# The w_sp product of a gMLP block, regrouped by one level of Strassen's scheme

## The chip, the cores and the metric

The kernel runs on one core of a Trainium2 chip. The core has TensorE (PE in the profile: matrix products into PSUM; its weight loads are listed as PEld), VectorE (DVE), ScalarE (ACT), GpSimd (POOL) and SyncE (SP), which here issues most of the DMAs. Each engine takes its instructions in order from a queue of its own; semaphores tie the queues together. The metric is the device time of one execution in microseconds (us); less is better.

## The reference

The module is a chain of two blocks with a residual around each. The first (an S4D convolution over 2048 positions, 512 channels) isn't touched by the change. The second is the gMLP mixer:

```python
def _B_ref(x, w_in, w_sp, b_sp, w_out):        # x: (1, 2048, 512), layer-normed
    Fh = F // 2                                 # F = 1792, Fh = 896
    z = _gelu(jnp.einsum("bsd,df->bsf", x, w_in))
    z1 = z[..., :Fh]
    z2 = _layernorm(z[..., Fh:], axis=-1)
    g = jnp.einsum("ts,bsf->btf", w_sp, z2) + b_sp[None, :, None]
    return jnp.einsum("bsf,fd->bsd", z1 * g, w_out)
```

The product in the line of g is the largest of the kernel: w_sp is 2048 x 2048, z2 is 2048 x 896. Everything is float32.

## The kernel before

**Stages.** The first block runs from the start of the profile to about 352 us; then phase_b1 (the rest of it, layer norm, transposes, and the half z1 of the first mixer product), phase_b2 (the other half, z2, with GELU and layer norm) and phase_b3 (the product with w_sp, the gate, the product with w_out, the stores). The change is in the end of phase_b2 and in phase_b3.

**Products in three parts.** A float32 operand is split into a rounded part `hi` and a remainder `lo`, both in a format (float32r) that TensorE takes at a higher rate. `split` (lines 917 to 919) is a cast on ScalarE and a subtraction on VectorE. A product is then hi·hi + hi·lo + lo·hi: three matmuls, which the loops over `((0, 0), (0, 1), (1, 0))` write out.

**phase_b2.** Row tile t of 16 (128 positions) gets two halves of 448 features (lines 1070 to 1079). After GELU and the statistics, lines 1083 to 1085 normalise each half in PSUM and split it into `z2[t]`, which holds hi and lo of 896 features. Twelve of the z2 tiles lie in the pool "z", four in the places of the earlier weights ("wa", "wb").

**phase_b3.** g is made transposed: 7 feature tiles (fb) of 128 features by 4 chunks (tch) of 512 output positions. For each chunk, 7 PSUM banks `gs` collect over 16 s-tiles (si) of 128 positions (lines 1151 to 1161). The weights held by TensorE are a 128 x 128 block of z2, the moving operand is a 128 x 512 block of w_sp. `raw(n)` loads such a block into one of 4 raw buffers, `wt(n)` splits it into one of 3 pairs, about 2 steps ahead. When a chunk is complete, its banks get b_sp (`bts`), are multiplied with z1, which is read back from DRAM (`z1s`), and split into `gz`: the gate (lines 1170 to 1183). While the next chunk runs, its steps 4, 7, 10 and 13 each take one block of 21 matmuls with w_out (`wo`), for 128 positions of the chunk before (lines 1162 to 1169); `store` adds the residual and writes the rows out. The last chunk's gate and product come at the end (lines 1186 to 1204); there the odd feature tiles are multiplied on GpSimd.

**Order.** In phase_b2 and phase_b3 the order in each engine's queue is set when the program is built, by a list scheduler that goes by the order of the text and by when it reckons operands to be ready: in the profile ScalarE casts w_out blocks between phase_b2's last tiles. PSUM has 7 banks under the tag "g" and one under "tp" (the blocks with w_out).

Of the kernel before, what the change touches and what calls it, by code (L numbers as in the profile page):

```python
# [22 lines left out]
NL2 = 64  # L23
# [154 lines left out]
class Plan:  # L178
# [738 lines left out]
def split(nc, hi, lo, src):  # L917
    nc.scalar.copy(hi, src)  # L918
    nc.vector.tensor_sub(lo, src, hi.bitcast(F32))  # L919
# [128 lines left out]
def phase_b2(tc, zp, wp, ins, ht, product, bank, mhalf):  # L1048

    nc = tc.nc  # L1050
    w2 = zp.tile([P, 2, 4, FH], F32R, tag="w2", name="w2")
    raw = [zp.tile([P, 2, FH], F32, tag="z", bufs=12, name=f"w2r{i}") for i in range(2)]
# [6 lines left out]
    z2 = [zp.tile([P, 4 * FQ], F32R, tag="z", bufs=12, name=f"z2_{t}") for t in range(12)]  # L1059
    for t in "wa", "wb":  # L1060
        ends = wp.tile([P, 2, 4 * FQ], F32R, tag=t, name=f"z_{t}")
        z2 += [ends[:, 0], ends[:, 1]]
    sms = zp.tile([P, 2, 16], F32, tag="sm", name="sm")
    for t in range(16):

        hi, lo = (ht[t // 4][k][:, :, P * (t % 4):P * (t % 4) + P] for k in range(2))
        sm = sms[:, t % 2]
        zt = z2[t].rearrange("p (k h f) -> p k h f", k=2, h=2)
        pts = []
        for half in range(2):  # L1070
            pt = bank(f"pz2_{t}_{half}", [P, 512])
            f = slice(FQ * half, FQ * half + FQ)
            for q in range(4):
                for i, (a, b) in enumerate(((hi, 0), (hi, 1), (lo, 0))):
                    nc.tensor.matmul(pt[:, :FQ], a[:, q], w2[:, b, q, f], start=(q == 0 and i == 0), stop=(q == 3 and i == 2))  # L1075
            v = pt[:, :FQ]
            nc.scalar.activation(v, v, AF.Gelu_apprx_tanh)
            nc.vector.bn_stats(sm[:, 6 * half:6 * half + 6], v)
# [10 lines left out]
def phase_b3(tc, hp, bp, ins, out, z2, w2, zos, bank, tp, scr):  # L1089

    nc = tc.nc
    z1_d, h_d = scr["z1"], scr["h"]
    NT = 4
    NW = 16 * NT

    def place(n, k, dt, name):
        t = hp.tile([P, 4, 512], dt, tag=f"h{n}{k}", name=name)
        return [t[:, i] for i in range(4)], [t[:, 2 * i:2 * i + 2] for i in range(2)]

    raws, _ = place(0, 0, F32, "raws")  # L1100
    sums = place(0, 1, F32, "sums0")[0] + place(1, 0, F32, "sums1")[0]
    z1s = [sums.pop(), zos[2]]
    wts = place(1, 1, F32R, "wts0")[1]
    w, g = place(2, 0, F32R, "wts1")[1]
    wts.append(w)
    gz = [t for n, k in ((2, 1), (3, 0), (3, 1)) for t in place(n, k, F32R, f"gz{n}{k}")[1]] + [g]
    gts = zos[:2]
    bts = [bp.tile([P, 512], F32, tag=f"bt{i}", name=f"bt{i}") for i in range(2)]
    NB = len(raws)

    def raw(n):
        if n < NW:
            nc.sync.dma_start(raws[n % NB], ins["w_sp"][n // 16, n % 16])

    def wt(n):
        if n < NW:
            split(nc, wts[n % 3][:, 0], wts[n % 3][:, 1], raws[n % NB])
            raw(n + NB)

    def load_b(tch):  # L1120
        nc.sync.dma_start(bts[tch % 2], ins["b_sp"].rearrange("(c o t) -> c o t", c=NT, o=1)[tch].to_broadcast([P, 512]))

    for k in range(NB):
        raw(k)
    wt(0)
    wt(1)
    wo = w2.rearrange("p k q f -> p k (q f)").rearrange("p k (b d) -> p k b d", d=D)
# [4 lines left out]
    for tch in range(2):  # L1132
        load_b(tch)


    ov = out.rearrange("b (a l) d -> (b l) a d", l=NL2)

    def load_h(tch, a, h):
        t0 = 512 * tch + P * a
        nc.sync.dma_start(h, h_d[t0:t0 + P])  # L1140

    def product(pt, a, fb):
        for i, (x, y) in enumerate(((0, 0), (0, 1), (1, 0))):
            nc.tensor.matmul(pt, gz[fb][:, x, P * a:P * a + P], wo[:, y, fb, :], start=(fb == 0 and i == 0), stop=(fb == FB - 1 and i == 2))  # L1144

    def store(tch, a, pt, h):
        nc.vector.tensor_add(h, pt, h)  # L1147
        l0 = 16 * tch + 4 * a
        nc.sync.dma_start(ov[l0:l0 + 4], h)

    for tch in range(NT):
        gs = [bank(f"g{tch}_{fb}", [P, 512]) for fb in range(FB)]
        for si in range(16):
            n = 16 * tch + si
            w = wts[n % 3]
            for fb in range(FB):
                if fb == 4:
                    wt(n + 2)
                f = slice(P * fb, P * fb + P)
                for i, (x, y) in enumerate(((0, 0), (0, 1), (1, 0))):  # L1160
                    nc.tensor.matmul(gs[fb], z2[si][:, x, f], w[:, y], start=(si == 0 and i == 0), stop=(si == 15 and i == 2))  # L1161
            if tch and si in (4, 7, 10, 13):
                a = (si - 4) // 3
                hr = gts[a % 2]
                load_h(tch - 1, a, hr)
                pt = tp(f"po{tch}_{si}", [P, 512])
                for fb in range(FB):
                    product(pt, a, fb)
                store(tch - 1, a, pt, hr)
        if tch < NT - 1:  # L1170
            bt = bts[tch % 2]
            for fb in range(FB):
                if fb % 2:
                    nc.scalar.copy(sums[fb], gs[fb])
                else:
                    nc.vector.tensor_add(sums[fb], gs[fb], bt)
            for fb in range(FB):
                z1 = z1s[fb % 2]
                nc.sync.dma_start(z1, z1_d[tch, fb])
                if fb % 2:  # L1180
                    nc.vector.tensor_add(sums[fb], sums[fb], bt)
                nc.vector.tensor_mul(sums[fb], sums[fb], z1)
                split(nc, gz[fb][:, 0], gz[fb][:, 1], sums[fb])
            if tch + 2 < NT:
                load_b(tch + 2)
    tch = NT - 1
    gl_, h4 = sums, list(gts)
    for a in range(2):
        load_h(tch, a, h4[a])
    for fb in range(FB):  # L1190
        nc.vector.tensor_add(gl_[fb], gs[fb], bts[tch % 2])  # L1191
    pl = [bank(f"pl{a}", [P, 512]) for a in range(4)]
    for fb in range(FB):
        z1 = z1s[fb % 2]
        nc.sync.dma_start(z1, z1_d[tch, fb])
        (nc.gpsimd if fb % 2 else nc.vector).tensor_mul(gl_[fb], gl_[fb], z1)  # L1196
        split(nc, gz[fb][:, 0], gz[fb][:, 1], gl_[fb])
        for a in range(4):
            product(pl[a], a, fb)
# [79 lines left out]
```

## Time and profile before

| | |
|---|---|
| runs | 952.91, 953.44, 953.70 us; median 953.44 |
| profiled execution | span 948.4 us, from the first to the last instruction; its own time isn't listed apart from the runs |
| mean granted TensorE clock | 0.983 |
| stage of the product with w_sp, gate and w_out | from 549.17 us to the end |
| DMA in the whole span | 88.86 MB, mean 94 GB/s |

How to read it: the span is taken by the hardware profiler on the core; the time of a run also holds what lies before the first instruction and after the last. A busy share is an average over stages with different limits, so the stages are read one by one, by windows. The chain that ended last is followed back from the last instruction to what released it.

### The profile page before, as it was taken

To read this page: it belongs to the slowest core of one execution; us is meant where nothing else is said; L and a number is where in the kernel's file an instruction comes from. 1 tells how busy PE (TensorE), PEld (TensorE's weight loads), DVE (VectorE), ACT (ScalarE), POOL (GpSimd) and SP (SyncE) were. 2 spreads that over 40 slices of the span, in tenths; PEclk is the share of its full clock that TensorE was granted. 3 is DMA by queue.
4 is the path that set the end of the run, shared out by engine and by line. 5 is a ranking of instruction groups with operands and counts; after the bars stand their busy time and mean duration, and the time that the engine had idled before them with its cause. 6 is when DMAs were issued, how large, how long until landed. Compare 5 with 4: busy or idle time off the path is not lost.

```text
span 948.4 us, 16818 instructions
## 1 busy us (share of the span) xinstructions
PE 857.6 (90%) x7000; PEld 730.3 (77%) x7000; DVE 525.8 (55%) x939; ACT 387.0 (41%) x623; POOL 241.6 (25%) x206
## 2 busy tenths in 40 slices
PE   1248799999999898899999999999999999999994
PEld 0137688888887898788899988888888888888883
DVE  6987979999988549564168751161116111611141
ACT  5876675887867331534344441131113111311010
POOL 5867475878766100000011100000000000000010
PEclk9999899999999999899999999999999999999997
DMA  9204410410403658452421032142224222422121
GB/s 358 67 1 143 89 28 23 102 31 27 100 2 80 223 226 227 134 135 95 179 72 34 12 111 56 56 128 77 74 67 130 71 78 67 125 74 79 45 69 54
DMA packets 45243, 88.86 MB, mean 94 GB/s; under 512 B 4464, under 2 KB 19568, under 8 KB 42736
## 3 DMA queue, kind: packets, MB, share of 16 engines
q1 hardware_dynamic: 43728, 85.17, 29.5%
q0 software_dynamic: 1440, 2.62, 1.1%
q8 instruction: 55, 0.90, 0.4%
q14 instruction: 20, 0.16, 0.1%
HBM read 59.99 MB, written 19.40 MB: 84 GB/s over the span
## 4 chain that ended last, share of the span: by engine, by line
PE 60%; DVE 1%; issue 0%; ACT 0%
PE g L1161 32%; PE pz L1026 8%; PE pz L1075 8%; PE po L1144 6%; PE y L992 3%; PE pl L1144 2%; DVE w1r L1015 0%; DVE w1r L1013 0%; PE lnh_pm L129 0%; DVE stats L997 0%; DVE raws L1147 0%; DVE xq L995 0%; DVE ht L919 0%; PE lnh_pv L138 0%; ACT big L486 0%
## 5 line engine op out<-in xcount | busy, mean ns | idle before, releaser
L1161 PE MATMUL g<-wts,z 128*128 128x512 f32 x1008 | 233.0, 391 | 0.0
L1161 PEld LDWEIGHTS g<-wts,z 128*128 128x128 f32 x1008 | 189.3, 188 | 41.5
L486 POOL TENSOR_TENSOR wa<-mt 128x512 f32<-128x512 f32 x96 | 149.5, 1581 | 63.8 <-PE ps L486 23.3
L919 DVE TENSOR_TENSOR wts<-raws,wts 128x512 fp32r<-128x512 f32 x64 | 44.1, 689 | 188.9 <-ACT wts L918 188.5
L918 ACT CAST wts<-raws 128x512 fp32r<-128x512 f32 x64 | 39.6, 620 | 256.9 <-PE g L1161 252.9
L1196 POOL TENSOR_TENSOR sums<-sums,zo 128x512 f32<-128x512 f32 x3 | 4.3, 1417 | 365.3 <-DVE sums L1191 359.2
L486 PE MATMUL ps<-big,a 128*128 128x128 f32 (+1 forms) x576 | 72.7, 283 | 11.1 <-ACT trio L486 8.5
L486 PEld LDWEIGHTS ps<-big,a 128*128 128x128 f32 x576 | 67.9, 195 | 15.4 <-ACT trio L486 8.7
L1075 PE MATMUL pz<-w,ht 128*128 128x448 f32 x384 | 77.4, 363 | 0.0
L1075 PEld LDWEIGHTS pz<-w,ht 128*128 128x128 f32 x384 | 72.0, 187 | 5.3
L1026 PE MATMUL pz<-ht,w1h 128*128 128x512 f32 x224 | 71.6, 399 | 0.0
L486 PE MATMUL ps<-c_inv,trio 128*128 128x128 f32 x512 | 62.4, 279 | 1.2 <-DVE f L486 1.1
L486 PEld LDWEIGHTS ps<-c_inv,trio 128*128 128x128 f32 x512 | 58.7, 192 | 4.2 <-DVE f L486 1.7
L486 ACT COPY big<-ps 128x512 f32<-128x512 f32 x74 | 42.8, 584 | 46.3 <-PE ps L486 45.0
L1081 POOL TENSOR_SCALAR sm<-sm 128x1 f32<-128x1 f32 x16 | 3.8, 238 | 223.0 <-DVE sm L1080 223.0
L1144 PE MATMUL po<-w,gz 128*128 128x512 f32 x216 | 52.2, 395 | 0.0
L1026 PEld LDWEIGHTS pz<-ht,w1h 128*128 128x128 f32 x224 | 42.8, 191 | 9.6
L486 ACT ACTIVATE ps<-wb 128x512 f32<-128x512 f32 x64 | 42.9, 687 | 17.0 <-DVE wb L486 15.9
L1144 PEld LDWEIGHTS po<-w,gz 128*128 128x128 f32 x216 | 40.6, 188 | 9.5
L486 DVE TENSOR_TENSOR trio<-ps,trio 128x1024 f32<-128x1024 f32 (+2 forms) x34 | 38.6, 1171 | 12.8 <-PE ps L486 12.7
L486 DVE SCALAR_TENSOR_TENSOR f<-wb,ps 128x1024 f32<-128x1024 f32 x32 | 38.8, 1217 | 12.2 <-ACT wb L486 12.0
L1026 PE MATMUL pz<-ht,w1l 128*128 128x512 f32 x112 | 45.0, 401 | 0.0
(146 smaller groups left out, 1376.0 us busy)
## 6 DMA issues: line engine op xcount, KB each, us to landing
raws<-in_w_sp_dram SPq DMA_DIRECT2D x64, 256.0 KB, 2.7
trio<-trio SPq DMA_DIRECT2D x8, 1024.0 KB, 11.9
g<-in_c_g_dram SPq DMA_DIRECT2D x8, 1024.0 KB, 4.9
scr_z<-zo SPq DMA_DIRECT2D x28, 256.0 KB, 2.0
big<-in_u_a_dram SPq DMA_DIRECT2D x8, 512.0 KB, 9.2
xq<-in_u_b_dram SPq DMA_DIRECT2D x4, 1024.0 KB
scr_h<-xq SPq DMA_DIRECT2D x16, 256.0 KB, 3.9
sums<-scr_z SPq DMA_DIRECT2D x16, 256.0 KB
```

The lines of the kernel that those rows point to most:

```text
L486: r = getattr(getattr(self.nc, e), method)(*[real(x) for x in args], **{k: real(x) for k, x in kw.items()})
L918: nc.scalar.copy(hi, src)
L919: nc.vector.tensor_sub(lo, src, hi.bitcast(F32))
L992: nc.tensor.matmul(py[:, i, :], gt[:, i, r, :], qv[:, r, l0 + i], start=(r == 0), stop=(r == 1))
L1026: nc.tensor.matmul(pt, w[:, q, f], ht[n][k][:, q], start=(q == 0 and i == 0), stop=(q == 3 and i == 2))
L1075: nc.tensor.matmul(pt[:, :FQ], a[:, q], w2[:, b, q, f], start=(q == 0 and i == 0), stop=(q == 3 and i == 2))
L1081: nc.gpsimd.tensor_scalar_add(sm[:, 14:15], sm[:, 13:14], 1e-5)
L1144: nc.tensor.matmul(pt, gz[fb][:, x, P * a:P * a + P], wo[:, y, fb, :], start=(fb == 0 and i == 0), stop=(fb == FB - 1 and i == 2))
L1161: nc.tensor.matmul(gs[fb], z2[si][:, x, f], w[:, y], start=(si == 0 and i == 0), stop=(si == 15 and i == 2))
L1196: (nc.gpsimd if fb % 2 else nc.vector).tensor_mul(gl_[fb], gl_[fb], z1)
```

## The change

The output chunks are taken in pairs p (chunks 2p and 2p + 1), the s-tiles in 8 pairs k (tiles 2k and 2k + 1, `e` and `o` in the code), the features in a left half (tiles 0 to 2, `S1`), a right half (4 to 6, `S2`) and a middle tile (3, `SE`). On these 2 x 2 blocks one level of Strassen's scheme is used: seven products of block sums take the place of eight products of blocks. Products 1, 2, 4 and 7 carry the middle tile along as a fourth feature tile, so that it is a plain product.

- `PRODUCTS` says which two blocks of w (chunk, s-tile) make the moving operand, with which sign, and to which chunk and feature tiles the result is added. `ORDERS` gives the order of the seven for each pair of chunks.
- `z2` is now kept in float32, 8 tiles of two row tiles each; the split in phase_b2 is gone.
- Each of the 112 steps (2 pairs, 7 products, 8 pairs of s-tiles) loads one or two w_sp blocks, sums two on GpSimd and splits the result (`w_prep`), and sums blocks of z2 (on GpSimd in products 3 and 4, on VectorE in 1, 6, 7) and splits that (`z_prep`). w is made 3 steps ahead, z 5. There are 6 raw buffers, 4 pairs for w and 8 for z.
- After each product, VectorE adds its 3 or 4 banks to the float32 sums `cs` (14 tiles, two chunks), the first time together with b_sp.
- `gate` is called as soon as feature tiles of a chunk are complete; its multiplication is on GpSimd (in chunk 3, odd tiles on VectorE).
- The blocks with w_out (`out_part`) wait in a list and are taken at steps 2 and 5 of a product, those of chunk 2 at steps 4 to 7. At the end, w_out's product with tiles 0 to 3 of the last chunk runs ahead of the last gate.

```diff
-        for half, v in enumerate(pts):
-            nc.vector.tensor_scalar(v, v, sm[:, 12:13], sm[:, 15:16], op0=ALU.subtract, op1=ALU.mult)
-            split(nc, zt[:, 0, half], zt[:, 1, half], v)
-    return [z.rearrange("p (k f) -> p k f", k=2) for z in z2], w2
+            o = z2[t // 2][:, t % 2, FQ * half:FQ * half + FQ]
+            nc.vector.tensor_scalar(o, v, sm[:, 12:13], sm[:, 15:16], op0=ALU.subtract, op1=ALU.mult)
+    return z2, w2
...
+S1, SE, S2 = slice(0, 384), slice(384, 512), slice(512, 896)
+LEFT, MID, RIGHT = range(0, 3), range(3, 4), range(4, 7)
+PRODUCTS = {
+    1: dict(w=((0, 0), (1, 1), 1), add=((0, LEFT, 1), (1, RIGHT, 1), (0, MID, 1))),
+    2: dict(w=((1, 0), (1, 1), 1), add=((1, LEFT, 1), (1, RIGHT, -1), (1, MID, 1))),
+    3: dict(w=((0, 0), None, 1), add=((0, RIGHT, 1), (1, RIGHT, 1))),
+    4: dict(w=((1, 1), None, 1), add=((0, LEFT, 1), (1, LEFT, 1), (0, MID, 1), (1, MID, 1))),
+    5: dict(w=((0, 0), (0, 1), 1), add=((0, LEFT, -1), (0, RIGHT, 1))),
+    6: dict(w=((1, 0), (0, 0), -1), add=((1, RIGHT, 1),)),
+    7: dict(w=((0, 1), (1, 1), -1), add=((0, LEFT, 1), (0, MID, 1))),
+}
+ORDERS = ((2, 3, 4, 6, 1, 5, 7), (1, 3, 4, 5, 7, 2, 6))
...
+    def w_prep(n):
+        p, m, k = steps[n]
+        hi, lo = wts[n % NW]
+        rs = mine[n]
+        if len(rs) == 2:
+            op = ALU.add if PRODUCTS[m]["w"][2] > 0 else ALU.subtract
+            nc.gpsimd.tensor_tensor(rs[0], rs[0], rs[1], op=op)
+        split(nc, hi, lo, rs[0])
+
+    def z_prep(n):
+        p, m, k = steps[n]
+        hi, lo = zcs[n % NZ]
+        e, o = z2[k][:, 0], z2[k][:, 1]
+        if m == 2:
+            split(nc, hi, lo, e[:, 0:512])
+            return
+        if m == 5:
+            split(nc, hi[:, :384], lo[:, :384], o[:, S2])
+            return
+        zs = zss[n % 2]
+        w = 512 if m == 4 else 384
+        x, y, op = {1: (e[:, S1], o[:, S2], ALU.add), 3: (e[:, S2], o[:, S2], ALU.subtract),
+                    4: (o[:, 0:512], e[:, 0:512], ALU.subtract), 6: (e[:, S1], e[:, S2], ALU.add),
+                    7: (o[:, S1], o[:, S2], ALU.add)}[m]
+        (nc.gpsimd if m in (3, 4) else nc.vector).tensor_tensor(zs[:, :w], x, y, op=op)
+        split(nc, hi[:, :w], lo[:, :w], zs[:, :w])
+        if m in (1, 7):
+            split(nc, hi[:, SE], lo[:, SE], (e if m == 1 else o)[:, SE])
...
+    def gate(tch, fbs):
+        for fb in fbs:
+            c, z1 = cs[tch % 2][fb], z1s[gated[0] % 2]
+            gated[0] += 1
+            nc.sync.dma_start(z1, z1_d[tch, fb])
+            (nc.vector if tch == 3 and fb % 2 else nc.gpsimd).tensor_tensor(c, c, z1, op=ALU.mult)
+            split(nc, gz[fb][0], gz[fb][1], c)
...
+    AHEAD_Z, AHEAD_W = 5, 3
...
+    for n, (p, m, k) in enumerate(steps):
+        if k == 0:
+            tiles = [x for x in (LEFT if m in (1, 2, 4, 7) else RIGHT)] + ([3] if m in (1, 2, 4, 7) else [])
+            ps = [bank(f"m{p}{m}_{i}", [P, 512]) for i in range(len(tiles))]
+        if n + AHEAD_Z < len(steps):
+            z_prep(n + AHEAD_Z)
+        if n + AHEAD_W < len(steps):
+            w_prep(n + AHEAD_W)
+            load_to(n + AHEAD_W + 2)
+        (whi, wlo), (zhi, zlo) = wts[n % NW], zcs[n % NZ]
+        for j, pt in enumerate(ps):
+            f = slice(P * j, P * j + P)
+            for i, (x, y) in enumerate(((zhi, whi), (zhi, wlo), (zlo, whi))):
+                nc.tensor.matmul(pt, x[:, f], y, start=(k == 0 and i == 0), stop=(k == KT - 1 and i == 2))
+        if todo and k in ((4, 5, 6, 7) if todo[0][0] == 2 else (2, 5)):
+            out_part(*todo.pop(0))
+        if k < KT - 1:
+            continue
+        for half, cols, sign in PRODUCTS[m]["add"]:
+            for i, fb in enumerate(cols):
+                pt, c = ps[3 if cols is MID else i], cs[half][fb]
+                if (p, half, fb) not in begun:
+                    begun.add((p, half, fb))
+                    nc.vector.tensor_tensor(c, bts[half], pt, op=ALU.add if sign > 0 else ALU.subtract)
                 else:
+                    nc.vector.tensor_tensor(c, c, pt, op=ALU.add if sign > 0 else ALU.subtract)
+        u = ORDERS[p].index(m)
+        if p == 0:
+            if m == 4:
+                gate(1, list(LEFT) + list(MID))
+            if m == 1:
+                gate(1, RIGHT)
+                todo += [(1, a) for a in range(4)]
+            if m == 7:
+                for tch in (2, 3):
+                    load_b(tch)
+                gate(0, range(FB))
+                todo += [(0, a) for a in range(4)]
+        else:
+            if m == 5:
+                gate(2, RIGHT)
+            if m == 7:
+                gate(2, list(LEFT) + list(MID))
+                todo += [(2, a) for a in range(4)]
+            if m == 2:
+                gate(3, list(LEFT) + list(MID))
+    tch = 3
     pl = [bank(f"pl{a}", [P, 512]) for a in range(4)]
+    hs = list(gts) + raws[:2]
+    for a in range(4):
+        load_h(tch, a, hs[a])
+    for a in range(4):
+        product(pl[a], a, range(0, 4), True, False)
+    gate(tch, RIGHT)
+    for a in range(4):
+        product(pl[a], a, range(4, 7), False, True)
+        store(tch, a, pl[a], hs[a])
```

More of the change, by code (lines that the diff above doesn't have):

```diff
@@ L1051, in phase_b2 @@
     w2 = zp.tile([P, 2, 4, FH], F32R, tag="w2", name="w2")
-    raw = [zp.tile([P, 2, FH], F32, tag="z", bufs=12, name=f"w2r{i}") for i in range(2)]
+    raw = [zp.tile([P, 2, FH], F32, tag="z", bufs=8, name=f"w2r{i}") for i in range(2)]
     for i in range(2):
@@ L1058, in phase_b2 @@
     product(3)
[L1059 to L1062, printed above, removed]
+    z2 = [zp.tile([P, 2, FH], F32, tag="z", bufs=8, name=f"z2_{k}") for k in range(8)]
     sms = zp.tile([P, 2, 16], F32, tag="sm", name="sm")
@@ L1067, in phase_b2 @@
         sm = sms[:, t % 2]
-        zt = z2[t].rearrange("p (k h f) -> p k h f", k=2, h=2)
         pts = []
@@ L1091, in phase_b3 @@
+ORDERS = ((2, 3, 4, 6, 1, 5, 7), (1, 3, 4, 5, 7, 2, 6))
+def phase_b3(tc, hp, bp, wp, ins, out, z2, w2, zos, bank, tp, scr):
     nc = tc.nc
     z1_d, h_d = scr["z1"], scr["h"]
-    NT = 4
-    NW = 16 * NT
+    KT = 8
     def place(n, k, dt, name):
         t = hp.tile([P, 4, 512], dt, tag=f"h{n}{k}", name=name)
-        return [t[:, i] for i in range(4)], [t[:, 2 * i:2 * i + 2] for i in range(2)]
-    raws, _ = place(0, 0, F32, "raws")
-    sums = place(0, 1, F32, "sums0")[0] + place(1, 0, F32, "sums1")[0]
@@ L1102, in phase_b3 @@
[L1102 to L1106, printed above, removed]
-    gts = zos[:2]
[L1108 to L1118, printed above, removed]
@@ L1120, in load_b, with twos @@
-    def load_b(tch):
[L1121 to L1127, printed above, removed]
+        return [t[:, i] for i in range(4)]
+    def twos(x):
+        return [(x[i], x[i + 1]) for i in range(0, len(x), 2)]
+    raws = place(0, 0, F32, "raws0")
+    x = place(0, 1, F32, "raws1")
+    raws, zss = raws + x[:2], x[2:]
@@ new lines, in phase_b3 @@
+    wts = twos(place(1, 0, F32R, "wts0") + place(1, 1, F32R, "wts1"))
+    x = []
+    for t in "wa", "wb":
+        v = wp.tile([P, 4 * FH], F32R, tag=t, name=f"zc_{t}")
+        x.append([v[:, 512 * i:512 * i + 512] for i in range(7)])
+    zcs = [(x[0][i], x[1][i]) for i in range(7)]
+    gz = twos(place(2, 0, F32R, "gz0") + place(2, 1, F32R, "gz1") + place(3, 0, F32R, "gz2") + place(3, 1, F32R, "gz3"))
+    zcs.append(gz.pop())
+    cs = [bp.tile([P, 512], F32, tag=f"c{i}", name=f"c{i}") for i in range(14)]
@@ new lines, in phase_b3 @@
+    cs = cs[:7], cs[7:]
+    bts = [bp.tile([P, 512], F32, tag=f"bt{i}", name=f"bt{i}") for i in range(2)]
+    z1s = [zos[2], bp.tile([P, 512], F32, tag="z1", name="z1b")]
+    gts = zos[:2]
+    NR, NW, NZ = len(raws), len(wts), len(zcs)
+    steps = [(p, m, k) for p in range(2) for m in ORDERS[p] for k in range(KT)]
+    loads = []
+    for n, (p, m, k) in enumerate(steps):
+        for blk in PRODUCTS[m]["w"][:2]:
+            if blk is not None:
+                loads.append((n, 2 * p + blk[0], 2 * k + blk[1]))
@@ new lines, in phase_b3, with load_to @@
+    mine = {}
+    for r, (n, _, _) in enumerate(loads):
+        mine.setdefault(n, []).append(raws[r % NR])
+    loaded = [0]
+    def load_to(n):
+        while loaded[0] < len(loads) and loads[loaded[0]][0] <= n:
+            r = loaded[0]
+            _, c, si = loads[r]
+            nc.sync.dma_start(raws[r % NR], ins["w_sp"][c, si])
+            loaded[0] += 1
+    def w_prep(n):
[6 more added lines that the diff above has]
+        split(nc, hi, lo, rs[0])
@@ new lines, in phase_b3, with load_h, product @@
+    wo = w2.rearrange("p k q f -> p k (q f)").rearrange("p k (b d) -> p k b d", d=D)
+    ov = out.rearrange("b (a l) d -> (b l) a d", l=NL2)
+    def load_b(tch):
+        nc.sync.dma_start(bts[tch % 2], ins["b_sp"].rearrange("(c o t) -> c o t", c=4, o=1)[tch].to_broadcast([P, 512]))
+    def load_h(tch, a, h):
+        t0 = 512 * tch + P * a
+        nc.sync.dma_start(h, h_d[t0:t0 + P])
+    def product(pt, a, fbs, first, last):
+        for fb in fbs:
+            for i, (x, y) in enumerate(((0, 0), (0, 1), (1, 0))):
+                nc.tensor.matmul(pt, gz[fb][x][:, P * a:P * a + P], wo[:, y, fb, :], start=(first and fb == fbs[0] and i == 0), stop=(last and fb == fbs[-1] and i == 2))
@@ new lines, in store, with out_part @@
+    def store(tch, a, pt, h):
+        nc.vector.tensor_add(h, pt, h)
+        l0 = 16 * tch + 4 * a
+        nc.sync.dma_start(ov[l0:l0 + 4], h)
+    gated = [0]
+    def gate(tch, fbs):
+        for fb in fbs:
+            c, z1 = cs[tch % 2][fb], z1s[gated[0] % 2]
[3 more added lines that the diff above has]
+            split(nc, gz[fb][0], gz[fb][1], c)
+    def out_part(tch, a):
+        hr = gts[a % 2]
+        load_h(tch, a, hr)
+        pt = tp(f"po{tch}_{a}", [P, 512])
+        product(pt, a, range(FB), True, True)
+        store(tch, a, pt, hr)
@@ L1128, in phase_b3 @@
+    AHEAD_Z, AHEAD_W = 5, 3
+    load_to(1)
+    for n in range(AHEAD_Z):
+        z_prep(n)
+        if n < AHEAD_W:
+            w_prep(n)
+            load_to(n + 2)
+    for tch in range(2):
+        load_b(tch)
     for fb in range(FB):
@@ L1131, in phase_b3 @@
         split(nc, wo[:, 0, fb], wo[:, 1, fb], t)
[L1132 to L1174, printed above, removed]
-                else:
[L1176 to L1191, printed above, removed]
-    pl = [bank(f"pl{a}", [P, 512]) for a in range(4)]
[L1193 to L1199, printed above, removed]
@@ L1200, in phase_b3 @@
-    h4 += raws[:2]
-    for a in range(2, 4):
-        load_h(tch, a, h4[a])
-    for a in range(4):
-        store(tch, a, pl[a], h4[a])
+    todo, begun = [], set()
+    for n, (p, m, k) in enumerate(steps):
+        if k == 0:
[21 more added lines that the diff above has]
+                    nc.vector.tensor_tensor(c, bts[half], pt, op=ALU.add if sign > 0 else ALU.subtract)
+                else:
+                    nc.vector.tensor_tensor(c, c, pt, op=ALU.add if sign > 0 else ALU.subtract)
[8 more added lines that the diff above has]
+                for tch in (2, 3):
+                    load_b(tch)
+                gate(0, range(FB))
[8 more added lines that the diff above has]
+                gate(3, list(LEFT) + list(MID))
@@ L1225, in body @@
         bp = es.enter_context(tc.tile_pool(name="b3", bufs=1, reuse_waits="tile"))
-        phase_b3(tc, hp, bp, ins, out, z2, w2, zos, bank, tp, scr)
+        phase_b3(tc, hp, bp, wp, ins, out, z2, w2, zos, bank, tp, scr)
 def layouts(v):
```

1 line of the change is left out of this document (removed).

## The prediction

> **What bounds the kernel now.** I read the page first: the span, the engines' shares and the chain that ended last.
>
> ```profile
> span 948.4 us, 16818 instructions
> PE 857.6 (90%) x7000; PEld 730.3 (77%) x7000; DVE 525.8 (55%) x939; ACT 387.0 (41%) x623; POOL 241.6 (25%) x206
> ...
> PE 60%; DVE 1%; issue 0%; ACT 0%
> ...
> L918 ACT CAST wts<-raws 128x512 fp32r<-128x512 f32 x64 | 39.6, 620 | 256.9 <-PE g L1161 252.9
> ```
>
> (The last row is a group of equal instructions: busy time, mean ns of one, idle time before it and what ended it. A cast of one w tile takes 0.62 us, and ScalarE waits for TensorE before it.) TensorE is busy for 90% of the span and nearly alone on the chain. The chain in order of time shows what it does in the stage that is changed, from 549.17 us on (count at the end of a row = matmuls):
>
> ```profile
> 471.93 77.24 PE pz L1075 x384
> 549.17 100.78 PE g L1161 x441
> 649.95 4.89 PE po L1144 x21
> 654.85 14.43 PE g L1161 x63
> 669.28 4.84 PE po L1144 x21
> ...
> 914.90 18.91 PE pl L1144 x81
> 933.81 0.03 issue
> 933.83 0.69 DVE raws L1147
> 934.52 0.00 issue
> 934.53 0.69 DVE raws L1147
> ```
>
> The product with w_sp (L1161) runs without a gap: 100.78 / 441 = 0.2285 us a matmul. A block of 21 po matmuls takes 4.89 or 4.84 us (I take 4.85). At the end two additions of 0.69 us stand bare. The windows by stage (us, then busy time of PE, PEld, DVE, ACT, POOL, then PE clock, DMA share, GB/s) show what else is there:
>
> ```profile
> 549.20:649.90 100.70, 100.70 (x442) 82.74 (x441) 35.21 (x57) 23.19 (x40) 0.77 (x2) 1.00 0.30 92
> 649.90:746.30 96.40, 96.40 (x422) 78.98 (x421) 26.47 (x41) 15.64 (x26) 0.00 (x0) 1.00 0.28 88
> ```
>
> VectorE is busy for 26 to 35 of 100 us and GpSimd does nothing. So a matmul less is time less here, until VectorE and GpSimd, to which the change gives work, become the bound. That is what the sum must decide.
>
> **TensorE.** Before, 4 chunks x 16 s-tiles x 7 feature tiles x 3 = 1344 matmuls. After, in each of two chunk pairs, products 1, 2, 4, 7 have 4 feature tiles and 3, 5, 6 have 3: 25 x 8 steps x 3 = 600, so 1200 in all, of the same shape. 144 x 0.2285 = **32.9 us** go. The 336 matmuls with w_out stay. At the end the stores of three row blocks now lie under the 9 matmuls of the next block, so one bare addition of 0.69 goes: -0.7. Nothing else could come off the floor, which is 948.4 - 33.6 = 914.8. A step of 12 matmuls lasts 2.74 us, one of 9 lasts 2.06.
>
> **The stage before (z2).** 32 casts and 32 subtractions leave it. The chain row of L1075 has 384 matmuls in 77.24 us with nothing between, so they were hidden: 0. They return inside the new loop, more than once.
>
> **The new vector work and its prices.** The durations come from the tail of before, the only place in this stage where GpSimd and VectorE work together (start, us, engine, operation):
>
> ```profile
> 912.15 0.68 DVE L1196 TENSOR_TENSOR sums<-sums,sums 128x512 f32<-128x512 f32 x1
> 912.31 1.68 POOL L1196 TENSOR_TENSOR sums<-sums,zo 128x512 f32<-128x512 f32 x1 [359.15 <-DVE sums L1191]
> 912.75 1.88 DVE L1191 TENSOR_TENSOR sums<-g,bt 128x512 f32<-128x512 f32 x3
> ...
> 915.74 0.68 DVE L919 TENSOR_TENSOR gz<-sums,gz 128x512 fp32r<-128x512 f32 x1
> 916.34 0.69 DVE L1196 TENSOR_TENSOR sums<-sums,sums 128x512 f32<-128x512 f32 x1
> ...
> 917.22 1.28 POOL L1196 TENSOR_TENSOR sums<-sums,zo 128x512 f32<-128x512 f32 x1 [3.23 <-DMA zo<-scr_z]
> ...
> 921.39 1.29 POOL L1196 TENSOR_TENSOR sums<-sums,zo 128x512 f32<-128x512 f32 x1 [2.89 <-DMA zo<-scr_z]
> 921.81 1.43 DVE L1196 TENSOR_TENSOR sums<-sums 128x512 f32<-128x512 f32 x1 [1.33 <-DMA sums<-scr_z]
> ```
>
> Three readings. A 512-wide VectorE operation follows the one before it after 0.60 us (915.74 to 916.34). A GpSimd operation takes 1.28 alone. And **the two do not run side by side when VectorE has both operands in SBUF**: at 921.81 VectorE started 0.42 into a GpSimd operation, and ended 0.56 after that one's end (922.68 to 923.24), taking 1.43 where 0.69 is usual; at 912.31 it was GpSimd that waited and took 1.68. The three additions from PSUM at 912.75 ran under that GpSimd operation at 0.63 each, undisturbed. The Trainium skill says the same on its page "SBUF — State Buffer", section "Who interferes with whom": a VectorE instruction with two SBUF inputs and a GpSimd instruction that reads SBUF exclude each other for the whole instruction, and one with a single SBUF input doesn't contend. The trace agrees, by the numbers above. By that rule the change is priced as below; without it each engine would keep up and the time would be the floor (rival A).
>
> Narrower forms, from these rows (448 wide on VectorE; GpSimd's least durations for 128 and 512):
>
> ```profile
> 550.42 0.62 DVE L919 TENSOR_TENSOR z_wb<-pz,z_wb 128x448 fp32r<-128x448 f32 x1
> 550.95 0.62 DVE L1078 BATCH_NORM_STATS2 sm<-pz 128x6 f32<-128x448 f32 x1
> ...
> L486 POOL TENSOR_TENSOR trio<-trio x10: 451/456/1450, 11.6 to 79.4; 128x128 f32<-128x128 f32 x6, 128x384 f32<-128x384 f32 x4
> L486 POOL TENSOR_TENSOR mt<-mt,rcs x8: 1261/1272/1816, 28.0 to 269.0; 128x512 f32<-128x512 f32 x8
> ```
>
> From 0.60 at 512 and 0.53 at 448 follow 0.45 at 384 and 0.15 at 128 on VectorE; from 0.451 and 1.261, about 1.0 at 384 on GpSimd. These are estimates.
>
> Each of the 112 steps now prepares its own w (a GpSimd addition of two blocks in products 1, 2, 5, 6, 7; a cast; a subtraction on VectorE) and its own z (a block sum on GpSimd in 3 and 4, on VectorE in 1, 6, 7; cast and subtraction). Time in which the pair is held, per step: product 1 and 7: 1.28 + 0.60 + 0.45 + 0.45 + 0.15 = 2.93; product 2: 1.28 + 0.60 + 0.60 = 2.48; 3: 0.60 + 1.0 + 0.45 = 2.05; 4: 0.60 + 1.28 + 0.60 = 2.48; 5: 1.28 + 0.60 + 0.45 = 2.33; 6: 1.28 + 0.60 + 0.45 + 0.45 = 2.78. A gate adds 1.28 + 0.60 = 1.88 a feature tile. Both pairs together: 2 x 143.8 + 25 x 1.88 = 335 us, against 2 x 137.1 + 12 x 4.85 = 332 us of TensorE. **The preparation is as long as the matmuls**, so it matters where it falls.
>
> On VectorE come the additions from PSUM, 3 to 8 after each product at 0.60, 41 a pair. They may lie under a GpSimd operation. Bounds: all of them hidden (x = 0), none (x = 1). The tail shows three hidden under one GpSimd operation, but GpSimd has often run ahead by then, as only the six raw buffers hold it back; I take half (x = 0.5).
>
> The account below goes from product to product, in the order of the code. W, the work while a product runs, is 5 of its own steps, 3 of the next one's (w is prepared 3 steps ahead), the additions and gates of the product before; the first has 7 splits of w_out (4.2). T is TensorE's time, with its blocks of w_out. A full lead is worth about 8 us (3 x 1.88 for w, 5 x 0.6 for z); it is spent first, and what is then short is a stall.
>
> | pair, product | T | W (x = 0.5) | lead left | stall |
> |---|---|---|---|---|
> | 0: 2 | 21.9 | 22.8 | 7.2 | 0 |
> | 0: 3 | 16.5 | 19.8 | 3.9 | 0 |
> | 0: 4 | 21.9 | 22.5 | 3.2 | 0 |
> | 0: 6 | 16.5 | 32.6 | 0 | 12.9 |
> | 0: 1 | 21.9 | 22.5 | 0 | 0.6 |
> | 0: 5 | 26.2 | 28.2 | 0 | 2.0 |
> | 0: 7 | 31.6 | 25.2 | 6.4 | 0 |
> | 1: 1 | 31.6 | 35.2 | 2.8 | 0 |
> | 1: 3, 4 | 48.1 | 41.0 | 8 | 0 |
> | 1: 5 | 16.5 | 22.8 | 1.6 | 0 |
> | 1: 7 | 21.9 | 29.5 | 0 | 6.0 |
> | 1: 2 | 41.3 | 29.5 | 8 | 0 |
> | 1: 6 | 16.5 | 23.5 | 1.0 | 0 |
>
> Product 6 of the first pair is worst: its own steps ask 2.78 against 2.06, and behind it lie 8 additions and the gate of 4 tiles from product 4; nothing of w_out is there yet to fill TensorE. Sum of stalls **21.5 us**; the same account with x = 0 gives 8.4, with x = 1 41.1. What queues behind a late VectorE operation is the next step's w, and behind that TensorE, in order.
>
> **DMA.** 192 loads of w_sp in place of 64:
>
> ```profile
> q1 hardware_dynamic: 17376, 31.99, 26.2%
> ...
> raws<-in_w_sp_dram SPq DMA_DIRECT2D x57, 256.0 KB, 2.7
> ```
>
> In the 399 us from 549 on, 31.99 MB took 26.2% of the 16 engines: full use would be 31.99 / (0.262 x 399) = 306 GB/s. Products 5 and 6 ask two blocks in 2.06 us, 524 KB, or 255 GB/s; 83%, so it fits. A raw buffer's round is 2.7 + 1.28 + 0.62 + 0.69 = 5.3 us for three steps, 1.8 a step; one blocked operation on each side (1.28 + 0.56) makes it 2.4. Bounds 0 to 32 steps x 0.3 = 10 us; I take 0, for the same waits are in the account. The tail: the 48 matmuls of tiles 0 to 3 (11 us) cover the last gate (about 0.7 + 1.3 + 0.6 + 0.7 for the first tile, 2 more tiles at 1.9: 7 us): 0, or up to 3 if the gate of tiles 0 to 3 is late.
>
> **Sum:** 948.4 - 32.9 - 0.7 + 21.5 = 936.3 of span. The median of the runs, 953.44, is 5.0 over the span of the profiled execution, whose own time isn't given apart; I keep the 5.0. **941 us.**
>
> **Rivals.** *A, the pair is no limit* (additions hidden, or the lock costs less): between 914.8 + 5.0 = 920 (VectorE and GpSimd each keep up, e.g. 8 x 1.28 + 5.1 = 15.4 of 16.5 us of GpSimd in product 6) and 920 + 8.4 = 928. For it: the three hidden additions. Against: the two waits in the tail. *B, slower: the additions from PSUM don't hide* because VectorE, in order, has one of its own two-operand subtractions blocked ahead of them: x = 1, 41.1 us of stalls, 920 + 41 = 961; it decides from a stall of 33.6, x = 0.8. For it: GpSimd's order puts its additions early, so it has nothing left when VectorE reads PSUM. Against: 912.75. *C, the loads or the gates hold the loop up* (z1 loads in SP's queue ahead of w_sp, two z1 buffers): the 10 of the DMA part on top of the forecast, 951: no change. *D, the change doesn't take matmuls away*: the count would show 1344; the code excludes it.
>
> **Chances.** Forecast (935 to 950) 0.46; A (920 to 935) 0.24; B (over 955.4) 0.24; C, near the old time, 0.06; D none. Hence faster 0.70, same 0.06, slower 0.24; 0.2% (1.9 us) is about what a measurement of this kernel can tell from no change. Of the range 924 to 964 I leave out the bare floor and what lies beyond x = 1.
>
> **What would show it.** L1161's successor with 1200 matmuls; TensorE idle before it, released by VectorE's or ACT's split, most in products 6 (first pair) and 7 (second); VectorE subtractions well above 0.69 and GpSimd above 1.28 on average; GpSimd busy for some 170 us after 549 (80 additions at 1.28, 8 x 2 x 2.28, 25 gates). It would be wrong if TensorE had no gaps (A), if GpSimd and VectorE kept their durations while TensorE waited for loads (C), or if the gaps sat at product ends, behind PSUM reads (B).

## The result: slower by 2.9%, and outside the range

The changed kernel takes 980.25 us in the median of 4 runs, against 953.33 for the kernel before (4 runs). The ratio is 1.0289, with a 95% interval of 1.0274 to 1.0303. The forecast was 941, the range 924 to 964: wrong in sign and in size.

The page of the changed kernel: span, engines, the chain that ended last, and three of the costliest groups (busy us, mean ns of one, idle time before it and what ended it).

```profile
span 978.7 us, 17579 instructions
PE 847.7 (87%) x6856; PEld 709.4 (72%) x6856; DVE 736.8 (75%) x1179; ACT 457.1 (47%) x774; POOL 443.2 (45%) x340
...
PE 33%; DVE 13%; DMA 5%; issue 5%; POOL 4%; ACT 1%; SPq 0%; POOLq 0%; DVEq 0%; ACTq 0%
...
L1247 PE MATMUL m<-wts,zc_wa 128*128 128x512 f32 x700 | 227.4, 400 | 18.4 <-DVE wts L919 17.8
L1158 POOL TENSOR_TENSOR raws<-raws 128x512 f32<-128x512 f32 x80 | 122.5, 1538 | 157.2 <-DMA raws<-in_w_sp_dram 156.8
...
L919 DVE TENSOR_TENSOR wts<-raws,wts 128x512 fp32r<-128x512 f32 x112 | 106.3, 951 | 19.1 <-ACT wts L918 18.8
```

TensorE held 60% of the chain before and holds 33% now; VectorE, DMAs and GpSimd stand in its place. A subtraction of w takes 0.951 us on average where it took 0.689, a GpSimd addition 1.538 where it takes 1.28 alone.

The windows of the stage (us, then busy time of PE, PEld, DVE, ACT, POOL, then TensorE's clock, DMA share, GB/s):

```profile
552.00:576.00 24.00, 24.00 (x106) 19.75 (x106) 22.54 (x31) 12.69 (x24) 12.98 (x10) 1.00 0.55 164
576.00:600.00 24.00, 23.73 (x103) 18.86 (x101) 23.86 (x29) 11.12 (x21) 11.08 (x7) 1.00 0.34 100
...
625.00:650.00 25.00, 23.41 (x86) 17.38 (x87) 24.97 (x29) 9.43 (x19) 14.58 (x10) 0.89 0.69 206
...
675.00:700.00 25.00, 20.65 (x78) 15.27 (x79) 25.00 (x33) 8.11 (x15) 11.57 (x8) 0.93 0.59 177
...
725.00:750.00 25.00, 17.17 (x67) 12.39 (x65) 11.53 (x16) 5.26 (x11) 10.45 (x9) 0.87 0.45 142
750.00:768.00 18.00, 15.46 (x54) 11.59 (x55) 15.68 (x12) 7.76 (x14) 17.51 (x12) 0.80 0.53 176
768.00:822.00 54.00, 54.00 (x237) 44.16 (x236) 39.33 (x60) 19.62 (x38) 18.05 (x13) 1.00 0.47 134
```

Three kinds of stretch can be told apart. From 576 to 600, 625 to 650 and 675 to 700 VectorE is hardly ever free. From 725 to 750 no engine is full: VectorE is busy for 12 of 25 us, TensorE for 17. From 750 to 768 GpSimd is full and TensorE runs at 0.80 of its clock. Where product 3 and then 4 run with few sums (768 to 822), TensorE has no gap.

**The balance.** I took the start of each of the 1536 matmuls of the stage from the trace. A step to the next start of under 300 ns counts as running; of 300 to 480 ns as half clock, with what is over 229 as loss; beyond that all over 229 is a gap. Before (1680 matmuls) 385.1 us were running and nothing else. After, 352.5 are running, 49.5 gaps, 13.7 half clock. So the 144 matmuls did go, 32.6 us (the forecast said 32.9), and 63.2 us of stalls came, where the forecast's account had 21.5. 63.2 - 32.6 = 30.6; the span grew by 30.3, the median of the runs by 26.9. That the first two agree so closely is partly luck: the stage starts 2.8 us later (551.83 against 549.01; the delay arose before phase_b2, whose 384 matmuls take 77.24 us in both), and what follows the start of its last matmul is 3.2 us shorter.

### The profile page after: what moved, and what is told of

Same layout as the page of the kernel before. It is cut to its first block, busy times and chain, and to the rows that moved or that the text cites. A ratio compares the mean times of both kernels' runs of the same rounds, so it can differ in the third digit from the quotient of the medians.

```text
span 978.7 us, 17579 instructions
## 1 busy us (share of the span) xinstructions
PE 847.7 (87%) x6856; PEld 709.4 (72%) x6856; DVE 736.8 (75%) x1179; ACT 457.1 (47%) x774; POOL 443.2 (45%) x340
## 4 chain that ended last, share of the span: by engine, by line
PE 33%; DVE 13%; DMA 5%; issue 5%; POOL 4%; ACT 1%; SPq 0%; POOLq 0%; DVEq 0%; ACTq 0%
PE m L1247 9%; PE pz L1026 8%; PE pz L1071 8%; PE po L1194 3%; DVE zc_wb L919 3%; DMA raws<-in_w_sp_dram 3%; DVE wts L919 3%; PE y L992 3%; POOL raws L1158 3%; PE pl L1194 2%; DVE c L1259 2%; DVE gz L919 2%; DVE raws L1176 2%; DMA out_dram<-zo 1%; POOL c L1209 1%
## 5 line engine op out<-in xcount | busy, mean ns | idle before, releaser
L1247 PE MATMUL m<-wts,zc_wa 128*128 128x512 f32 x700 | 227.4, 400 | 18.4 <-DVE wts L919 17.8
L1158 POOL TENSOR_TENSOR raws<-raws 128x512 f32<-128x512 f32 x80 | 122.5, 1538 | 157.2 <-DMA raws<-in_w_sp_dram 156.8
L1247 PEld LDWEIGHTS m<-wts,zc_wa 128*128 128x128 f32 x700 | 134.0, 191 | 55.8 <-DVE wts L919 26.7
L1247 PE MATMUL m<-wts,zc_wb 128*128 128x512 f32 x350 | 138.7, 397 | 0.0
L919 DVE TENSOR_TENSOR wts<-raws,wts 128x512 fp32r<-128x512 f32 x112 | 106.3, 951 | 19.1 <-ACT wts L918 18.8
L918 ACT CAST wts<-raws 128x512 fp32r<-128x512 f32 x112 | 69.2, 619 | 108.0 <-POOL raws L1158 95.4
L1247 PEld LDWEIGHTS m<-wts,zc_wb 128*128 128x128 f32 x350 | 67.1, 192 | 13.7
L919 DVE TENSOR_TENSOR zc_wb<-raws,zc_wa 128x384 fp32r<-128x384 f32 (+1 forms) x70 | 66.0, 945 | 12.6 <-ACT zc_wa L918 12.4
L918 ACT CAST zc_wa<-raws 128x384 fp32r<-128x384 f32 (+1 forms) x70 | 37.3, 534 | 75.4 <-PE m L1247 43.0
L1176 POOL TENSOR_TENSOR raws<-z 128x384 f32<-128x384 f32 (+1 forms) x32 | 47.9, 1495 | 34.0 <-DVE zc_wb L919 23.3
```

The costliest lines, as they stand in the source:

```text
L1158: nc.gpsimd.tensor_tensor(rs[0], rs[0], rs[1], op=op)
L1176: (nc.gpsimd if m in (3, 4) else nc.vector).tensor_tensor(zs[:, :w], x, y, op=op)
L1247: nc.tensor.matmul(pt, x[:, f], y, start=(k == 0 and i == 0), stop=(k == KT - 1 and i == 2))
```

## The experiments

Theory L: VectorE and GpSimd shut each other out. Theory S: the SyncE queue stands still behind the stores. Theory G: the blocks with w_out stand in TensorE's queue before their gate is ready. Rivals are named at each. The kernel before took 953.18 us beside experiments 1 to 4 and 953.00 beside 5 to 8.

### 1. All sums and gate products on VectorE

```diff
-            nc.gpsimd.tensor_tensor(rs[0], rs[0], rs[1], op=op)
+            nc.vector.tensor_tensor(rs[0], rs[0], rs[1], op=op)
...
-        (nc.gpsimd if m in (3, 4) else nc.vector).tensor_tensor(zs[:, :w], x, y, op=op)
+        nc.vector.tensor_tensor(zs[:, :w], x, y, op=op)
...
-            (nc.vector if tch == 3 and fb % 2 else nc.gpsimd).tensor_tensor(c, c, z1, op=ALU.mult)
+            nc.vector.tensor_tensor(c, c, z1, op=ALU.mult)
```

> All GpSimd work of the loop (80 w sums, 30 z sums, 25 gate products) moves to VectorE; nothing else. In the changed kernel TensorE stood 49.5 us in gaps and lost 13.7 more at half clock, of 978.7. Theory L (VectorE and GpSimd shut each other out while both have two SBUF operands): a 512-wide sum costs 0.60 on VectorE where it cost it 1.28 of standing still, so the product windows come to 17 to 27 us of VectorE against 16.5 to 41 of TensorE, the stalls of the SyncE queue stay (about 20 with their half clock): 940 to 955. Rival V (VectorE is simply full, 737 us busy, and GpSimd was relief): 135 more operations at 0.6 make it slower, 1000 or above.

Measured: 941.33 us, ratio to the kernel before 0.9874 (0.986 to 0.9889). That is 38.9 us less than the changed kernel, by giving the busiest helper 137 operations more. VectorE is then busy for 723 us of the span, less than the 737 with GpSimd's help. Gaps 16.7, half clock 6.0. L holds, V falls. GpSimd's sums also took longer than VectorE's, so the chain load, sum, cast, subtraction got shorter too; experiment 5 tells the two apart.

### 2. Residual rows in buffers of their own

```diff
-        hr = gts[a % 2]
+        hr = {0: cs[0][4:] + gts[:1], 1: cs[1], 2: cs[0]}[tch][a]
...
-    hs = list(gts) + raws[:2]
+    hs = gts[1:] + cs[0][4:]
```

The sums of a chunk are free between its gate and the next pair, so they can hold the residual.

> The residual rows no longer go through the two buffers whose store has to land first: the free tiles of cs are used, so that no load of h waits 6 us at the head of the SyncE queue with the w_sp loads behind it (61.4 us of such waits in 12 places in the changed kernel). Theory S: the empty stretches at 700 to 768 and 909 to 949 shrink and with them some half clock: 955 to 965. Theory L alone: VectorE is full in 576 to 600, 625 to 700 and 822 to 888 and those stay; if the SyncE waits lie beside that, 976 to 982.

Measured: 972.05 us, ratio 1.0196 (1.018 to 1.0211): 8.2 less, between the two expectations. The mechanism is in the trace of the changed kernel; first its SyncE queue in order of time (start, us, what), then its chain of waits at that place, then what the queue waited for in all (us, times, longest):

```profile
722.93 0.55 SPq L1199 DMA_DIRECT2D out_dram<-zo  x1
728.89 0.33 SPq L1189 DMA_DIRECT2D zo<-scr_h  x1
729.31 9.61 SPq L1149 DMA_DIRECT2D raws<-in_w_sp_dram  x6
```

```profile
722.93 5.94 DMA out_dram<-zo
...
729.31 2.96 DMA raws<-in_w_sp_dram
...
732.34 0.61 POOL raws L1158
```

```profile
SPq L1149 <- POOL raws L1158: 96.8, 58, 6.3
SPq L1149 <- DVE wts L919: 90.3, 63, 3.9
SPq L1189 <- DMA out_dram<-zo: 61.4, 12, 6.2
```

A store of output rows lands after 5.94 us. The next instruction of the queue loads h into the same buffer, so it waits for that, and the w_sp load behind it goes out 6.4 us late; GpSimd idles until it has landed. The experiment takes these 12 waits away and saves 8.2 us of the 61.4; the rest had lain beside other waits or came back as such (the queue's waits for `DVE wts` grew from 90.3 to 113.0 us).

### 3. Both

> Both edits at once. If L and S are separate and are all of it: the floor of TensorE, 980.25 - 63 = 917, plus a few us where additions from PSUM and gates meet: 918 to 930, faster than the kernel before. If S is only a consequence of L (late buffers make the loads late): about what the sums on VectorE alone give. If a third cause is left (the matmul order, the loads' rate): above 935.

Measured: **933.60 us, ratio 0.9785 (0.9768 to 0.9802)**: with them the scheme is faster than the kernel before. 46.7 us less than the changed kernel, where the single edits gave 38.9 + 8.2 = 47.1: the effects of the two edits add up. It ended a little above the range expected, with 11.1 us of gaps and 5.1 of half clock left. TensorE runs without a gap where VectorE has room, and loses where VectorE is full (windows of this kernel, as above):

```profile
625.00:650.00 25.00, 23.88 (x100) 17.90 (x99) 24.59 (x49) 12.98 (x27) 0.00 (x0) 1.00 0.75 237
650.00:675.00 25.00, 22.69 (x92) 17.96 (x91) 23.63 (x45) 10.73 (x21) 0.00 (x0) 0.93 0.69 202
...
775.00:800.00 25.00, 25.00 (x111) 20.53 (x111) 18.07 (x36) 9.94 (x22) 0.00 (x0) 1.00 0.49 142
```

From 625 to 650 VectorE does 49 operations in 25 us; with GpSimd's help it did 29 in the same window.

### 4. Without the accumulation

```diff
-                else:
-                    nc.vector.tensor_tensor(c, c, pt, op=ALU.add if sign > 0 else ALU.subtract)
```

> Of the 82 additions from PSUM on VectorE only the first into each sum is kept, 54 are left out (so most of the product sums are missing); GpSimd work and SyncE queue as in the changed kernel. 54 x 0.60 = 32 us of VectorE go. If those additions are not covered in the stretches where VectorE is full (x = 1 of the prediction): 15 to 25 us less, 955 to 965. If they lie under GpSimd operations (x = 0): 976 to 981.

Measured: 966.39 us, 13.9 less than the changed kernel: 0.26 us for each of the 54 additions, of the 0.60 that one takes. Both expectations were missed; the answer lies between them. It can't be turned into the share x of the prediction. The stalls moved: product 6 of the first pair lost 13.7 us where it had lost 8.6, product 5 of the second 13.5 where it had lost 2.2, and products 1, 2 and 6 of the second fell to 6.7, 0 and 0. Nor does the prediction's account lose the whole of each addition that lies open, as part of it goes into the lead: redone without these 54, it falls by 7.7 us for x = 0.5 and by 21.9 for x = 1. So x isn't known. But even with x = 1 the account gives 41.1 us of stalls where 63.2 were measured, so x alone is not where the forecast failed.

### 5. A bystander on GpSimd

Experiment 3 took work from GpSimd and shortened the chain load, sum, cast, subtraction. This one, built on experiment 3, gives GpSimd work on which nothing depends.

```diff
+    def idle(n):
+        w = 384 if steps[n][1] in (3, 5, 6) else 512
+        v = zcs[n % NZ][0][:, :w].bitcast(F32)
+        nc.gpsimd.tensor_tensor(gts[0][:, :w], v, v, op=ALU.add)
...
             z_prep(n + AHEAD_Z)
+            idle(n + AHEAD_Z)
```

(The fourth residual row of chunk 0 goes into the other of the two buffers, so that `gts[0]` is free.)

> The kernel with both edits (all sums on VectorE, own residual buffers; 933.6) plus one GpSimd addition a step that nobody needs: it adds the newest z block to itself into a tile that is read by no one, 112 of them, 512 or 384 wide. No instruction waits for it but the next use of that z buffer, 8 steps later. Theory L (exclusion of the two engines): each of them holds VectorE off for 1.0 to 1.2 us, about 130 us in all, where VectorE is busy 314 of 384 us already: VectorE's subtractions of w go from 0.69 to 0.85 or more on average, and the time to 948 to 965. Rival C (what cost time in the changed kernel was the longer chain load, sum on GpSimd, cast, subtraction; the engines don't hold each other up): 932 to 936 and 0.69.

Measured: 968.66 us, 35.1 more than experiment 3 and a little over the range expected. There are 107 bystanders, not 112, as the first five steps prepare their z ahead of the loop. The groups of experiment 3, then of this one (VectorE's subtraction of w and its addition from PSUM; GpSimd's bystander):

```profile
L919 DVE TENSOR_TENSOR wts<-raws,wts 128x512 fp32r<-128x512 f32 x108 | 74.1, 687 | 2.1 <-ACT wts L918 1.9
...
L1259 DVE TENSOR_TENSOR c<-c,m 128x512 f32<-128x512 f32 x54 | 35.0, 681 | 1.2 <-PE m L1247 1.2
```

```profile
L919 DVE TENSOR_TENSOR wts<-raws,wts 128x512 fp32r<-128x512 f32 x108 | 88.0, 816 | 0.8 <-ACT wts L918 0.8
...
L1265 DVE TENSOR_TENSOR c<-c,m 128x512 f32<-128x512 f32 x54 | 34.8, 675 | 0.9 <-PE m L1253 0.9
...
L1222 POOL TENSOR_TENSOR zo<-zc_wa 128x512 f32<-128x512 f32 x51 | 104.3, 2046 | 85.7 <-ACT zc_wa L918 73.6 <-DMA raws<-in_w_sp_dram 10.0
L1222 POOL TENSOR_TENSOR zo<-zc_wa 128x384 f32<-128x384 f32 x42 | 68.3, 1625 | 51.0 <-ACT zc_wa L918 49.0
```

VectorE's subtraction goes from 0.687 to 0.816 us, GpSimd's own 512-wide operation takes 2.05 on average, where 1.28 is what it takes alone; a few very long ones make that mean (see the last section). The addition from PSUM, which reads only one operand from SBUF, keeps its 0.68. In all VectorE is busy for 774 us where it was busy for 724, with the same operations. The bystander's own hold on its z buffer is not it: ScalarE waited for that twice, 1.7 us in all. So the mutual exclusion by itself costs TensorE 36 us here (stalls of 52.4 against 16.2), and C falls.

### 6 and 7. The blocks with w_out later

```diff
-        if todo and k in ((4, 5, 6, 7) if todo[0][0] == 2 else (2, 5)):
+        if k in {(0, 5): (6,), (0, 7): (1, 3, 5), (1, 3): (3, 6), (1, 5): (1, 4), (1, 2): (4, 5, 6, 7)}.get((p, m), ()):
```

Experiment 6 is this alone; experiment 7 is this with the two edits of experiment 3, and with the last residual rows in sums that are free by then.

> The changed kernel with the w_out blocks taken at other steps only: those of chunk 1 in product 5 at step 6 and in product 7 at 1, 3, 5, those of chunk 0 in product 3 at 3, 6 and in product 5 at 1, 4 (one and two products later). Theory G (in the first product of the second pair TensorE waited because the blocks stood in its queue ahead of their gate): the 15.6 us lost there shrink to under 6, and the blocks fill TensorE where VectorE is behind: 965 to 973. Rival: VectorE's and the loads' arrears are only moved to the next product: 977 to 983.

> Both edits and the later blocks. In the kernel with both edits TensorE still lost 16.2 us, 3.6 of them in the first product of the second pair, 4.9 in its product 7 and 4.6 in product 5 of the first. Theory G: 922 to 929. Rival: 932 to 936.

Measured: 983.36 us (ratio 1.0331, 1.0312 to 1.035) and 939.39 (0.9859, 0.9844 to 0.9874): 3 more than the changed kernel, and 6 more than experiment 3; the first just above the rival's range, the second above both ranges. In the first product of the second pair of experiment 6 TensorE lost 14.8 us where it had lost 15.6. In the changed kernel its two longest waits there stood before blocks (3.71 and 6.18 us, for `gz`); with the blocks a product later it waited nearly as long in all, now for the split of w. The blocks' place in the text is not what cost the time; theory G falls.

### 8. Only the sums of w on VectorE

The first of the three edits of experiment 1.

> Of the work that the first experiment moved, only the 80 sums of w go to VectorE; z sums and gate products stay on GpSimd. Theory L: they are 122 of the some 205 us that GpSimd was busy in this stage, so about 60% of the 39 us that all of it gave: 954 to 960. If the z sums and gates, few but in bursts, are what blocks: above 968. If the sums of w alone do it: below 946.

Measured: 960.69 us (ratio 1.0101, 1.0059 to 1.0143; five runs from 956.85 to 968.95), 19.6 less than the changed kernel, half of what all three edits give, and just over the range expected. The other half belongs to 57 operations out of 137, so z sums and gate products cost more apiece. That they come in bursts would explain it, but wasn't tried by itself. Products 1, 2 and 6 of the second pair, which cost 34.0 us in the changed kernel and 6.6 in experiment 1, still cost 27.9 here. In the changed kernel GpSimd was busy for 17.51 of 18 us from 750 to 768, where a gate of 7 tiles, sums of w and sums of z stand one behind the other.

## Why the prediction was wrong

Stalls by product, gaps and half clock together, from the starts of the matmuls (us; the products are told apart by counting the 1200 matmuls):

| pair: product | account (x = 0.5) | changed kernel | 1: sums on VectorE | 2: own buffers | 3: both |
|---|---|---|---|---|---|
| 0: 2, 3, 4 | 0 | 0.9 | 0 | 1.0 | 0 |
| 0: 6 | 12.9 | 8.6 | 1.0 | 8.7 | 1.0 |
| 0: 1 | 0.6 | 3.0 | 2.2 | 3.1 | 2.0 |
| 0: 5 | 2.0 | 4.8 | 4.3 | 4.9 | 4.6 |
| 0: 7 | 0 | 4.1 | 2.3 | 2.2 | 0 |
| 1: 1 | 0 | 15.6 | 6.6 | 12.5 | 3.6 |
| 1: 3, 4, 5 | 0 | 2.2 | 0.4 | 1.5 | 0 |
| 1: 7 | 6.0 | 5.6 | 5.9 | 5.6 | 4.9 |
| 1: 2 | 0 | 7.7 | 0 | 8.3 | 0 |
| 1: 6 | 0 | 10.7 | 0 | 5.4 | 0 |
| sum | 21.5 | 63.2 | 22.7 | 53.3 | 16.2 |

- **Right: the floor.** 144 matmuls less are 32.6 us; the stage before hid its lost splits, as said.
- **Two small terms.** The -0.7 was misread: TensorE's last matmuls before ended at 934.49, so only the second of the two additions stood bare, and one does so after. The 5.0 us between span and run is 1.9 in the changed kernel (980.58 and 978.7) and 1.7 to 1.9 in every run that is listed with its span; 948.4 belongs to an execution of some 950.3 (estimated so).
- **Right: the mechanism that limits.** The two engines exclude each other, and experiment 5 shows it with work that nobody needs. The account, made of that alone, put 18.9 of its 21.5 us into product 6 of the first pair and product 7 of the second; there it measured 14.2. Its signs came true in the durations (0.951 and 1.538 us, GpSimd busy for 196 us where 170 were said), but not in the places: 49 of the 63.2 us lie elsewhere. The choice x = 0.5 was neither confirmed nor refuted.
- **Wrong: the term of 21.5 us of stalls, by 42.** Four fifths of what was missed (34 of 42) lie in three products that the account gave a lead and no stall: 1, 2 and 6 of the second pair. Even with x = 1 it gives them only 1.3. There it failed in two steps. One was the step "T is TensorE's time, with its blocks of w_out": it compared two totals, that of TensorE with its blocks and that of the pair of engines, as if work of either could fill any gap. But GpSimd takes its gates and sums one behind the other, at 1.5 us apiece; with all of that on VectorE these three products cost 6.6 in place of 34.0. With only the sums of w moved they still cost 27.9, so most of it comes with the gates and z sums. How much is their order and how much the exclusion, no run separates.
- **Wrong: "DMA ... I take 0".** It looked at rates and buffers, and not at the SyncE queue, in which the loads stand behind the stores. The store and the load behind it stand in the trace of the kernel before, too, 5.98 us apart:

```profile
655.60 0.67 SPq L1149 DMA_DIRECT2D out_dram<-zo  x1
661.58 0.33 SPq L1140 DMA_DIRECT2D zo<-scr_h  x1
662.01 9.01 SPq L1113 DMA_DIRECT2D raws<-in_w_sp_dram  x3
```

  With one load in 4.8 us and four raw buffers nobody noticed; with two in 2.06 to 2.74 us they cost 8.2. The longest stall of the changed kernel, 7.98 us before 932.15 in product 6 of the second pair, stands at the end of such a wait (its chain, start, us, what):

```profile
915.68 6.85 DMA out_dram<-zo
...
922.97 2.91 DMA z1b<-scr_z
...
926.01 1.27 POOL c L1209
...
927.71 3.00 DMA zo<-scr_z
...
930.80 0.06 DVE c L1209
...
931.41 0.69 DVE zo L1197
...
932.15 7.77 PE po L1194 x21
```

  After the store has landed, the load of h goes out, and behind it the z1 of a gate; GpSimd's product makes room for the next z1, VectorE's product waits for that one, and the residual addition behind it frees the PSUM bank for TensorE's next block. Experiment 2 halves the stalls of this product (10.7 to 5.4), experiment 1 ends them with the store waits still there, so GpSimd's work and the queue both have a hand in it. This is rival C's queue, with its z1 loads and its two z1 buffers; its price, at most 10 us, was near the 8.2, but it was put on top of a forecast that was too low.
- **Not in the account: the half clock.** 13.7 us by the sorting above, of which 10.1 are steps of 0.42 to 0.43 us and the rest single steps of 0.32 to 0.37 just behind a gap. They come with the gaps: 12.4 in experiment 2, 6.0 in 1, 5.1 in 3.
- **Rival B** had the sign and 961 us, for another reason (x = 1). Experiment 4 doesn't refute that x, though the 13.9 us it saved fall short of the 21.9 that x = 1 would have given; but where the time went speaks against B, as the 34.0 us above are 1.3 in its account.

What stays open: which part of the 16.2 us left in experiment 3 is VectorE's sheer load and which the order of its queue. It loses most in the products with the fullest VectorE windows, but that was only read, not tried. Open as well is x, the share of the additions from PSUM that costs time.

## What to carry to other kernels

Before giving GpSimd a share of VectorE's work, ask whether both will have two SBUF operands. A GpSimd sum takes 1.28 us, in which such a VectorE operation stands still, and VectorE does that sum itself in 0.60; here it was busy for longer with the helper (737 us) than without (723). Two engines that share a resource can't be summed and compared with a third: follow the order of each queue through the fullest stretch. When loads become three times as many, read the queue that issues them for every wait that was harmless so far, a store and a load on the same buffer above all.

## What the runs showed of the hardware that was not expected

**GpSimd can be shut out for far longer than one instruction.** In the changed kernel (in order of time; GpSimd's row merges two additions, the first of which took 7.04 us by the chain of waits):

```profile
602.78 8.28 POOL L1158 TENSOR_TENSOR raws<-raws 128x512 f32<-128x512 f32 x2 [9.12 <-DMA raws<-in_w_sp_dram]
```

```profile
603.01 0.54 DVE L919 TENSOR_TENSOR zc_wb<-raws,zc_wa 128x384 fp32r<-128x384 f32 x1
603.48 0.28 DVE L919 TENSOR_TENSOR zc_wb<-z,zc_wa 128x128 fp32r<-128x128 f32 x1
603.68 0.55 DVE L919 TENSOR_TENSOR zc_wb<-raws,zc_wa 128x384 fp32r<-128x384 f32 x1
...
608.10 0.55 DVE L1176 TENSOR_TENSOR raws<-z 128x384 f32<-128x384 f32 x1
610.49 1.11 DVE L919 TENSOR_TENSOR wts<-raws,wts 128x512 fp32r<-128x512 f32 x1 [1.84 <-ACT wts L918]
```

From 602.41 to 608.65 VectorE runs 14 operations with two SBUF operands back to back, none longer than usual. The GpSimd addition, the next w that TensorE needs, ends at 609.82, some 1.2 us after VectorE pauses. In experiment 5 the median of 93 of the 107 bystanders is 1.205 us, and the longest took 13.3 us (least, median, most, in ns):

```profile
L1222 POOL TENSOR_TENSOR zo<-zc_wa x93: 824/1205/13342, 563.6 to 904.4; 128x512 f32<-128x512 f32 x51, 128x384 f32<-128x384 f32 x42
```

The Trainium skill's page "SBUF — State Buffer", section "Who interferes with whom", says that whoever issues first gets the shared pair for the whole instruction. The trace agrees for a single instruction: VectorE's subtraction at 610.49 takes 1.11 us beside GpSimd's second addition, which ends at 611.06. It shows besides that GpSimd got no turn between the 14 instructions of VectorE, which followed without a break.

**Half clock after short gaps.** TensorE's rows of the changed kernel after a thin stretch (the last two start 0.43 us apart, in place of 0.2285):

```profile
623.53 0.91 PE L1194 MATMUL po<-w,gz 128*128 128x512 f32 x2 [1.91 <-ACT gz L918]
625.30 0.80 PE L1247 MATMUL m<-wts,zc_wa 128*128 128x512 f32 x1 [0.86 <-DVE wts L919]
625.89 0.63 PE L1247 MATMUL m<-wts,zc_wb 128*128 128x512 f32 x1
626.32 0.63 PE L1247 MATMUL m<-wts,zc_wa 128*128 128x512 f32 x1
```

The granted clock from 625 to 650 was 0.89. No single gap here was longer than 2.1 us, but three of 0.9, 2.1 and 1.2 us came between 618 and 626. A gap of 8 us (before 932.15) and one of 6 (before 751.93) had the same sequel.
